# Another order of work for a gated mix of linear attention and a squared-ReLU layer

## Chip, cores and metric

The kernel runs on one core of a Trainium2 chip. The metric is the device time in microseconds (us) of one execution. Of the core's engines four compute here: TensorE (PE in the profile, with its weight loads as PEld), VectorE (DVE), ScalarE (ACT) and GpSimd (POOL). SyncE (SP) issues most of the DMAs.

## The reference

For 2048 rows `x` of width 448 in float32, the output mixes two branches row by row:

```python
g = sigmoid((x * gate_w).sum(-1, keepdims=True))
q, k, v = split(x @ wqkv)                     # 16 heads of 28
phi = lambda t: where(t > 0, t + 1, exp(t)) + 1e-6
kv  = einsum("bhsd,bhse->bhde", phi(k), v)    # sum over all 2048 rows
z   = sum of phi(k) over the rows
a   = (phi(q) @ kv / (phi(q) . z + 1e-6)) @ wo
b   = square(relu(x @ w1 + b1)) @ w2 + b2     # hidden width 1792
out = g * a + (1 - g) * b
```

The kernel does not form `v`. It sums `x^T phi(k)` over the rows (the "gram") and multiplies that by the `v` part of the weights once, then folds `kv` and `wo` into one matrix `m`.

## The kernel before

**Splitting.** A matrix product in float32 is made of three products of shorter numbers: each operand is split into a high part (rounded to `fp32r`) and a low part (what is left). Making the high part is a copy with a change of type (`split_hi`, lines 460 to 466); making the low part is a subtraction with two inputs (`split_lo`, line 468), which VectorE or GpSimd does.

**Two streams.** Every matmul uses 64 rows of the array, the lower half (`LO`) or the upper half (`UP`). Two streams of matmuls, one for each half, therefore run side by side. Both may add into the same bank of PSUM, but not at once. There are eight banks: four `acc` (outputs `o_ps` of the hidden layer's second product), two `mm` (first product, `h_ps`) and two `ms` (all else).

**Tiling and stages.** The rows are worked on in four blocks of 512 (`b` = 0 to 3) and 16 tiles of 128 (`t`); the hidden layer in 14 pieces of 128 columns (`f`). The first half of the kernel takes, for each block, the pieces 0 to 6 (`up` into `h_ps`, `hidden` on the other engines, `down` into `o_ps`), four key tiles (`keys`, `k_ps`) and four products of the gram (`gram`, `g_ps`). Between the halves stand `key_sums` (`z_ps`), `kv_product` (`kv_ps`) and `m_product` (`m_ps`), whose result goes through 32 DMAs on the POOL queue to `m_s`. The second half takes the blocks in the order 3, 0, 1, 2: pieces 7 to 13, the queries (`q_ps`), the denominators (`d_ps`) and the attention (`a_ps`).

**What follows each bank.** `hidden` (line 611) does ReLU and square on ScalarE, the high part on VectorE (`split_hi(dve, ...)`) and the low part on VectorE. `keys_done` (line 692) does an exponential, two VectorE operations for `phi`, the split of the key tile into `ph` and `pl`, adds the tile to `ksum` on GpSimd, and splits the raw `x` tile into `nh` and `nl`, with both subtractions on GpSimd (lines 700 to 709). `queries_done` (line 882) does `phi` and adds to the sum for the denominator; `denominators` (line 912) takes four reciprocals on VectorE and then splits the four query tiles (`scaled`).

**Who sets the order.** The class `Flow` is a planner that runs while the program is being written down. A call such as `dve.tensor_tensor(...)` only puts an operation into a list (`queue`, line 205), with an estimated duration (`cost`, line 218) and a rank (line 211: the planned time plus the patience of the step). `candidate` (line 235) picks for each engine, among the first 60 waiting operations, the one that can start first, and among equals the lowest rank. `product` (line 331) picks the next job of each matmul stream, looking up to 12 jobs ahead. The main loop (`run`, line 374) always carries out the earliest event. So the planner's estimates decide in which order each engine's instructions stand in the program. On the chip each engine then keeps that order and waits by semaphores; the planned times themselves have no effect there. The constants that feed the plan are on lines 32 to 34: time of one matmul of 512 or 448 columns, and the time from an engine's end to another's start.

**The first four products.** Line 991 gives the first four pieces of `h_ps` their banks: two from `mm`, and two from `ms`.

Of the kernel before, what the change touches and what calls it, by code (L numbers as in the profile page):

```python
# [16 lines left out]
P = 128  # L17
# [17 lines left out]
AFTER = mybir.DependencyInfo(mybir.DependencyClass.Sync, mybir.DependencyReason.DATA)  # L35

# [27 lines left out]
class Op:  # L64


    def __init__(self, emit, cost, after, rank, takes=None, size=0):
        self.emit, self.cost, self.after, self.rank = emit, cost, after, rank
        self.takes, self.size, self.end = takes, size, None

# [54 lines left out]
class Flow:  # L125
# [4 lines left out]
    def __init__(self, tc):  # L130
        self.tc, self.nc = tc, tc.nc
        self.tiles, self.queues, self.free, self.holds, self.kept, self.readers, self.shapes = {}, {}, {}, {}, {}, {}, {}
        self.now, self.patience, self.dma, self.switched = 0.0, 0.0, 1.3, -1.0
# [30 lines left out]
    def engine(self, name, unit):  # L164
# [3 lines left out]
        class Proxy:  # L168
            def __getattr__(self, method):
                return lambda *args, **kwargs: flow.queue(name, getattr(unit, method), method, args, kwargs)  # L170
        return Proxy()

# [32 lines left out]
    def queue(self, name, method, kind, args, kwargs):  # L205
        aps = [x for x in (*args, *kwargs.values()) if isinstance(x, View) or hasattr(x, "tensor")]
        out = kwargs.get("out", args[0] if args else None)
        parts = [(x, x is out) for x in aps]
        op = Op(lambda: method(*[real(x) for x in args], **{k: real(x) for k, x in kwargs.items()}),  # L209
                self.cost(name, kind, out, [x for x in aps if x is not out], args),  # L210
                {o for x, writes in parts for o in self.meeting(x, writes)}, self.now + self.patience,
                out.hold if isinstance(out, View) else None, free_size(out) * list(like(out).ap)[0][1] * 4
                if kind == "dma_start" else 0)
        for x, writes in parts:
            self.note(x, op, writes)
        self.queues[name].append(op)

    def cost(self, name, kind, out, ins, args):
        n = free_size(out)
        ps = any(like(x).space == PSUM for x in ins)  # L220
        wide = sum(free_size(x) > 1 for x in ins)
        if kind == "dma_start":
            return 0.54 if name == "pool" else 0.06
        if name == "act":
            f = args[2] if len(args) > 2 else None
            return {AF.Relu: 0.26, AF.Exp: 0.18}.get(f, 0.25 if ps and f else 0.205) + n * 0.000835
        if name == "pool":
            return 0.25 + n * 0.002 if wide > 1 else 0.4 + n * 0.001
        if kind == "reciprocal":
            return 0.13 + n * 0.006  # L230
        if kind == "memset":
            return 0.1
        return 0.155 + n / 960 if wide > 1 or ps else 0.1 + n * 0.00064

    def candidate(self, name):
        best = None
        for k, op in enumerate(self.queues[name][:60]):
            if any(x.end is None for x in op.after):
                continue
            start = max([self.free[name], self.now] + [x.end + SIGNAL for x in op.after])  # L240
            if op.takes is not None and op.takes.buffer is None:
# [3 lines left out]
                start = max(start, v[0])  # L245
            key = (max(start, self.free[name] + 0.05), op.rank)
            if best is None or key < best[0]:
                best = key, start, k
        return best and best[1:]

    def dispatch(self, name, k, start):
        op = self.queues[name].pop(k)
# [3 lines left out]
        self.tc.keep_in_program_order(op.emit())  # L256
        self.free[name] = op.end = start + op.cost
        if op.size:
            self.dma = max(self.dma, start + 0.6) + op.size / 385e3
            op.end = self.dma + LANDING  # L260

    def ready(self, j, s):
# [10 lines left out]
        if j.ready[s] is None:  # L275
# [3 lines left out]
            j.ready[s] = max([op.end + SIGNAL for op in wrote], default=0.0)  # L279
# [8 lines left out]
    def empty(self, tag):  # L288

        found = []  # L290
        for n, b in enumerate(self.banks[tag]):
            if b is None:
                found.append((0.0, n))
            elif b.end is not None:
                ops = [op.end for _, op, _ in self.tiles[b.ps.tensor.name]]
                if None not in ops:
                    found.append((max(ops) + SIGNAL, n))
        return min(found, default=None)

    def emit(self, j, s):  # L300
# [23 lines left out]
        if b.seen == b.total:  # L324
            b.end = self.stream[s]
            op = Op(None, 0.0, (), 0.0)
            op.end = b.end + LATE
            self.note(b.ps, op, True)
            b.done()
# [18 lines left out]
    def enter(self, n):  # L348
        while self.entered <= n + 1 and self.entered < len(self.steps):
            self.entered += 1  # L350
            self.patience = self.steps[self.entered - 1].patience
            if self.steps[self.entered - 1].before:
                self.steps[self.entered - 1].before()
# [834 lines left out]
```

## Time and profile before

| | us |
|---|---|
| median of 3 executions | 440.71 (440.56 to 440.78) |
| the profiled execution, its own time | 441.48 |
| span of the profiled execution, first to last instruction | 439.7 |

The span leaves 441.48 - 439.7 = 1.78 us of the execution's time outside. The granted clock of TensorE was 1.000 of full speed over the whole span. How to read the views: a matmul's record lasts longer than its share of the array, as two streams overlap, so the busy time of PE says little about how dense the matmuls are. The weight loads (PEld) are shorter, one for each matmul. In the timeline a row stands for one instruction or a run of like ones, and the brackets show what ended the idle time before.

### The profile page before, as it was taken

The page shows a single profiled execution, that of the slowest core. Times are in us where ns is not written, and L with a number is a line of the kernel's source. Part 1 is how long each engine was busy: PE and PEld are TensorE (multiplying, and loading weights), DVE is VectorE, ACT ScalarE, POOL GpSimd, SP SyncE. Part 2 cuts the span into 40 slices and gives each one's busy share as a digit, 9 for nine tenths or more (in the row PEclk, how much of TensorE's full clock was granted, in tenths as well). Part 3 has the DMA queues.
Part 4 walks back from the last instruction along what each step waited for, and adds up shares of the span by engine and source line. Part 5 has one row for each costly group of instructions (what it writes and reads, how often), then busy time and mean ns, then how long its engine had stood idle before and what let it go on. Part 6 is the DMA issues. An engine that isn't in the chain of part 4 may idle for free.

```text
span 439.7 us, 9349 instructions
## 1 busy us (share of the span) xinstructions
PE 433.8 (99%) x3978; PEld 413.3 (94%) x3978; DVE 268.5 (61%) x454; ACT 172.2 (39%) x298; POOL 67.5 (15%) x91
## 2 busy tenths in 40 slices
PE   8999999999999999999999999999999999999996
PEld 6899999999999999989999999999999899998995
DVE  4798525753587416783555849949535983458624
ACT  5846324532254214561533526415324242322530
POOL 0134104510065002530004900000000000000000
PEclk9999999999999999999999999999999999999999
DMA  7652210040111302223124631011210210001002
GB/s 255 240 152 87 76 46 25 23 138 25 41 59 45 113 3 66 83 84 92 41 86 112 110 92 49 0 64 34 62 49 1 85 25 1 0 33 55 1 1 83
DMA packets 17994, 29.02 MB, mean 66 GB/s; under 512 B 2544, under 2 KB 12448, under 8 KB 17952
## 3 DMA queue, kind: packets, MB, share of 16 engines
q1 hardware_dynamic: 16544, 26.81, 19.6%
q0 software_dynamic: 1408, 1.61, 2.2%
q8 instruction: 31, 0.51, 0.5%
q14 instruction: 11, 0.09, 0.1%
HBM read 22.08 MB, written 3.67 MB: 59 GB/s over the span
## 4 chain that ended last, share of the span: by engine, by line
PE 91%; DVE 5%; ACT 1%; DMA 1%; issue 0%; SPq 0%; DVEq 0%; ACTq 0%
PE h_ps L310 31%; PE o_ps L310 28%; PE a_ps L310 8%; PE g_ps L310 8%; PE k_ps L310 7%; PE q_ps L310 7%; DVE slot L209 4%; ACT slot L209 1%; PE kv_ps L310 1%; DMA slot<-in_xt 1%; DVE q L209 1%; PE m_ps L310 1%; PE d_ps L310 0%; ACT x L209 0%; PE z_ps L310 0%
## 5 line engine op out<-in xcount | busy, mean ns | idle before, releaser
L310 PE MATMUL h_ps<-x,w 64*128 64x512 f32 x1176 | 257.3, 394 | 0.4 <-ACT x L209 0.3
L310 PE MATMUL o_ps<-w_all,slot 64*128 64x448 f32 (+1 forms) x1332 | 240.5, 363 | 0.4 <-DVE slot L209 0.4
L310 PEld LDWEIGHTS o_ps<-w_all,slot 64*128 64x128 f32 (+1 forms) x1332 | 205.7, 184 | 6.5 <-DVE slot L209 1.8
L310 PEld LDWEIGHTS h_ps<-x,w 64*128 64x128 f32 x1176 | 193.6, 185 | 7.5 <-ACT x L209 0.8
L209 ACT ACTIVATE slot<-h_ps,few 128x512 f32<-128x512 f32 x56 | 38.0, 686 | 95.8 <-PE h_ps L310 83.8
L310 PE MATMUL q_ps<-x,wq_s 64*128 64x512 f32 x308 | 74.3, 393 | 0.0
L310 PE MATMUL k_ps<-wkm,x 64*128 64x450 f32 x336 | 66.3, 364 | 0.0
L209 DVE TENSOR_TENSOR slot<-slot,slot 128x512 fp32r<-128x512 f32 (+2 forms) x85 | 61.3, 733 | 4.4 <-DMA slot<-slot 1.7
L310 PE MATMUL a_ps<-wkm,q 64*128 64x448 f32 x336 | 62.2, 361 | 0.1
L310 PEld LDWEIGHTS k_ps<-wkm,x 64*128 64x128 f32 x336 | 57.0, 185 | 1.4 <-ACT slot L209 0.2
L310 PEld LDWEIGHTS q_ps<-x,wq_s 64*128 64x128 f32 x308 | 55.1, 184 | 1.5 <-DVE slot L209 0.3
L310 PEld LDWEIGHTS a_ps<-wkm,q 64*128 64x128 f32 x336 | 53.8, 184 | 1.3 <-DVE slot L209 0.6
L310 PE MATMUL g_ps<-p,nh 64*128 64x448 f32 x256 | 54.5, 359 | 0.0
L209 ACT ACTIVATE slot<-slot 128x512 f32<-128x512 f32 (+2 forms) x69 | 42.4, 625 | 14.7 <-DVE slot L209 13.8
L209 DVE CAST slot<-slot 128x512 fp32r<-128x512 f32 (+1 forms) x58 | 24.9, 430 | 31.9 <-ACT slot L209 30.7
L310 PEld LDWEIGHTS g_ps<-p,nh 64*128 64x128 f32 x256 | 40.6, 184 | 0.5
L209 POOL TENSOR_TENSOR nl<-slot,nh 128x384 fp32r<-128x384 f32 x16 | 19.3, 1209 | 117.6 <-ACT nh L209 117.6
L310 PE MATMUL g_ps<-p,nl 64*128 64x448 f32 x96 | 32.0, 360 | 0.0
L209 DVE SCALAR_TENSOR_TENSOR part<-part,gate,slot 128x448 f32<-128x448 f32 x13 | 8.8, 683 | 31.2 <-ACT slot L209 31.2
L209 ACT ACTIVATE slot<-a_ps,gate 128x448 f32<-128x448 f32 x16 | 10.0, 634 | 42.7 <-PE a_ps L310 40.7
L209 POOL TENSOR_TENSOR ksum<-ksum,slot 128x448 f32<-128x448 f32 x15 | 19.7, 1314 | 27.6 <-DVE slot L209 23.0
L209 DVE SCALAR_TENSOR_TENSOR slot<-slot,slot 128x448 f32<-128x448 f32 (+1 forms) x32 | 22.0, 688 | 1.7 <-ACT slot L209 1.5
(69 smaller groups left out, 350.0 us busy)
## 6 DMA issues: line engine op xcount, KB each, us to landing
slot<-in_xt SPq DMA_DIRECT2D x27, 256.0 KB, 2.8
slot<-in_xn SPq DMA_DIRECT2D x16, 224.0 KB, 2.5
out<-slot SPq DMA_DIRECT2D x16, 224.0 KB, 1.9
slot<-in_w SPq DMA_DIRECT2D x14, 224.0 KB, 2.8
slot<-in_w1a SPq DMA_DIRECT2D x8, 256.0 KB, 2.8
slot<-in_w1b SPq DMA_DIRECT2D x8, 192.0 KB, 4.0
wkm<-m POOLq DMA_DIRECT2D x24, 56.0 KB, 2.4
slot<-in_wq SPq DMA_DIRECT2D x4, 256.0 KB, 2.6
```

What stands on the lines that cost most here:

```text
L209: op = Op(lambda: method(*[real(x) for x in args], **{k: real(x) for k, x in kwargs.items()}), self.cost(name, kind, out, [x for x in aps ...
L310: ins = pe.matmul(b.ps[where or b.whole], real(a), real(m), start=b.seen == 1 + j.whole, stop=b.seen == b.total)
```

## The change

- **Three tables.** `SHIFT` adds to the rank of every operation that a bank or a step brings about (key: the bank's name or the step's), `MOVE` sorts the jobs of both matmul streams by step number plus an entry, `LEAVE` sets how willingly a copy goes to VectorE.
- **Copies to either engine.** `split_hi`, the copy of the query tile `c == 3` and the first copy into `gsum` are queued for ScalarE and VectorE at once (`either`); `candidate` compares when each would end, with 0.3 us (or the table's entry) added for VectorE. Whichever takes it removes it from the other's list. This holds for the copies of `hidden` too, which VectorE had, and for the other splits, which ScalarE had.
- **Key tiles.** The addition to `ksum` and both subtractions for `nl` and `nh` go from GpSimd to VectorE. GpSimd keeps the clearing and copies of `key_sums` and its DMAs.
[...]
- **Banks.** The third and fourth piece of the first four take `acc` banks instead of `ms` banks.
- **Conditions for the moved jobs.** `key_sums` waits for all key banks, `kv_product` for all gram banks, and a product that reads a block of `x` waits until all four chunks of it have been queued for splitting (`whole_x`).

The diff, cut to its core (each table with a few of its entries):

```diff
-C512, C448 = 0.2305, 0.204
+C512, C450, C448 = 0.2325, 0.2055, 0.2025
-LATE, SIGNAL, LANDING, HANDED = 0.25, 0.08, 1.9, 0.4
+LATE, SIGNAL, TO_PE, LANDING, HANDED = 0.17, 0.035, 0.09, 1.7, 0.22
+OVERLAP = {"act": 0.1, "dve": 0.085, "pool": 0.05, "sp": 0.0}
+SHIFT = {"a_ps1": 1.5, "a_ps10": 3, "a_ps13": -7.5, "d_ps1": 14.5, "g_ps0_0": 35, "k_ps1": 16, "k_ps10": 27.5,
...
+MOVE = {"a_ps10": 1.5, "a_ps11": -2.5, "a_ps12": 0.5, "a_ps14": 2.5, "a_ps9": 2.5, "d_ps0": 1, "d_ps1": -1.5,
+    "d_ps2": -0.5, "k_ps2": -5, "k_ps10": -3, "q_ps2_0": -4, "q_ps2_1": -3.5,
...
+LEAVE = {"a_ps10": 0.15, "a_ps14": -0.3, "h_ps0_0": 0.6, "h_ps0_1": 1, "h_ps0_10": 0, "k_ps0": 0.6,
...
+    def either(self, **calls):
+        self.queue({name: (getattr(unit, method), method, args, kwargs)
+                    for name, (unit, method, args, kwargs) in calls.items()})
...
+        op = Op({n: way(n, *call) for n, call in calls.items()},
+                {o for x in aps for o in self.meeting(x, x is out)},
+                self.now + self.patience + SHIFT.get(self.label, 0.0),
...
+        op.leave = LEAVE.get(self.label, 0.3)
...
+            if op.ways[name][2]:
+                start = max(start, self.port["pool" if name == "dve" else "dve"])
...
+        if best is not None and len(best[4].ways) > 1:
+            key, start, k, _, op, ready = best
+            ends = {n: max(ready, self.free[n]) + op.ways[n][1] + (op.leave if n == "dve" else 0.0) for n in op.ways}
+            best = key, start + ends[name] - min(ends.values()), k, start
...
-        self.jobs = [[(n, j) for n, step in enumerate(steps)
-                      for j in step.jobs[step.turn * s:] + step.jobs[:step.turn * s]] for s in range(2)]
+        self.jobs = [sorted([(n, j) for n, step in enumerate(steps)
+                             for j in step.jobs[step.turn * s:] + step.jobs[:step.turn * s]],
+                            key=lambda x: x[0] + MOVE.get(x[1].bank.name, 0.0)) for s in range(2)]
...
+    def copy(to, src):
+        flow.either(act=(nc.scalar, "activation", (to, src, AF.Copy), {}), dve=(nc.vector, "tensor_copy", (to, src), {}))
+
     def split_hi(eng, hi, src):
-        if eng is act:
-            act.activation(hi, src, AF.Copy)
-        elif eng is pool:
-            pool.tensor_scalar(hi, src, 1.0, 0.0, op0=ALU.mult, op1=ALU.add)
-        else:
-            eng.tensor_copy(hi, src)
+        copy(hi, src)
...
-        if t == 0:
-            pool.tensor_copy(ksum, p)
+        if not pend:
+            dve.tensor_copy(ksum, p)
         else:
-            pool.tensor_tensor(ksum, ksum, p, op=ALU.add)
+            dve.tensor_tensor(ksum, ksum, p, op=ALU.add)
...
-        split_lo(pool, nl, raw[:, :384], nh[:, :384])
-        split_lo(pool, nh[:, D:], raw[:, 384:], nh[:, 384:D])
+        split_lo(dve, nl, raw[:, :384], nh[:, :384])
+        split_lo(dve, nh[:, D:], raw[:, 384:], nh[:, 384:D])
...
-                act.copy(gsum[c], bank.ps[:, :D])
+                copy(gsum[c], bank.ps[:, :D])
...
-            act.copy(v, ps)
+            copy(v, ps)
...
-    first = [up_bank(0, f, *((mm_p, "mm") if f < 2 else (ms_p, "ms"))) for f in range(4)]
+    first = [up_bank(0, f, *((mm_p, "mm") if f < 2 else (acc_p, "acc"))) for f in range(4)]
```

More of the change, by code (lines that the diff above doesn't have):

```diff
@@ L64, with __init__ @@
 class Op:
-    def __init__(self, emit, cost, after, rank, takes=None, size=0):
-        self.emit, self.cost, self.after, self.rank = emit, cost, after, rank
+    def __init__(self, ways, after, rank, takes=None, size=0):
+        self.ways, self.after, self.rank = ways, after, rank
         self.takes, self.size, self.end = takes, size, None
+        self.leave = 0.0
 class Hold:
@@ L203, in note, with queue, way @@
                 x.hold.uses.append(op)
-    def queue(self, name, method, kind, args, kwargs):
+    def queue(self, calls):
+        (name, (_, kind, args, kwargs)), *_ = calls.items()
         aps = [x for x in (*args, *kwargs.values()) if isinstance(x, View) or hasattr(x, "tensor")]
         out = kwargs.get("out", args[0] if args else None)
[L208 to L211, printed above, removed]
+        n = next(k for k, x in enumerate(aps) if x is out)
+        ins = aps[:n] + aps[n + 1:]
+        def way(name, method, kind, args, kwargs):
+            return (lambda: method(*[real(x) for x in args], **{k: real(x) for k, x in kwargs.items()}),
+                    *self.cost(name, kind, out, ins, args))
+        op = Op({n: way(n, *call) for n, call in calls.items()},
+                {o for x in aps for o in self.meeting(x, x is out)},
+                self.now + self.patience + SHIFT.get(self.label, 0.0),
@@ L227, in cost @@
         if name == "pool":
-            return 0.25 + n * 0.002 if wide > 1 else 0.4 + n * 0.001
+            return 0.25 + n * 0.002 if wide > 1 else 0.4 + n * 0.001, wide > 0
         if kind == "reciprocal":
-            return 0.13 + n * 0.006
+            return 0.13 + n * 0.0063, False
         if kind == "memset":
-            return 0.1
-        return 0.155 + n / 960 if wide > 1 or ps else 0.1 + n * 0.00064
+            return 0.1, False
+        plain = not ps and all(len([k for _, k in list(like(x).ap)[1:] if k > 1]) < 2 for x in (out, *ins))
@@ L235, in candidate @@
+        if wide > 1 or not plain:
+            return 0.06 * scaled + 0.155 + n / 960, wide > 1 and not ps
+        return 0.06 * scaled + 0.093 + n * 0.00064, n > 8
     def candidate(self, name):
@@ L239, in candidate @@
                 continue
-            start = max([self.free[name], self.now] + [x.end + SIGNAL for x in op.after])
+            ready = max([self.now] + [x.end + SIGNAL for x in op.after])
+            start = max(self.free[name], ready)
             if op.takes is not None and op.takes.buffer is None:
@@ L278, in ready @@
                 return None
-            j.ready[s] = max([op.end + SIGNAL for op in wrote], default=0.0)
+            j.ready[s] = max([op.end + TO_PE for op in wrote], default=0.0)
         t = max([self.stream[s], j.ready[s], self.left.get((o, j.bank), 0.0)] + [x.end for x in j.after])
@@ L605, in whole_up @@
         low, high = [], []
+        if x_key(b, f) not in whole_x:
+            raise KeyError
         for c in range(4):
@@ L689, in keys @@
         bank.done = lambda: keys_done(t, bank.ps)
-        return [Job(bank, lambda: key_terms(t), C448, [("x", t // 4, False), "wk"])]
+        return [Job(bank, lambda: key_terms(t), C450, [("x", t // 4, False), "wk"])]
     def keys_done(t, ps):
@@ L775, in key_sums_job @@
         bank.done = lambda: sums_done(bank.ps)
-        return [Job(bank, key_sums, 0.07, ["zk"], [key_banks[NT - 1]])]
+        return [Job(bank, key_sums, 0.224, ["zk"], list(key_banks.values()))]
     kv, wv_s, kvm = [], [], []
@@ L818, in kv_product @@
     def kv_product():
-        return [Job(kv_bank, kv_terms, 0.19, ["wv"], [grams[NB - 1, c] for c in range(4)])]
+        return [Job(kv_bank, kv_terms, 0.196, ["wv"], list(grams.values()))]
     wo_raw, wo_s = {}, {}
```

67 lines of the change are left out of this document (44 added, 23 removed), and 44 rows, old and new, of tables (LEAVE, MOVE, SHIFT).

## The prediction

> **What bounds the kernel now.** I read the page's busy times and chain first.
>
> ```profile
> PE 433.8 (99%) x3978; PEld 413.3 (94%) x3978; DVE 268.5 (61%) x454; ACT 172.2 (39%) x298; POOL 67.5 (15%) x91
> ...
> PE 91%; DVE 5%; ACT 1%; DMA 1%; issue 0%; SPq 0%; DVEq 0%; ACTq 0%
> ```
>
> TensorE is the bound: 91% of the chain of work that ended last is matmuls, and the number of matmuls is the same after the change. So a gain can only come from stretches in which the two streams of matmuls are thinner than they could be. PE's 99% hides these, because records of the two streams overlap: while one stream waits, the other still shows as busy. The view of windows shows them, by the count and busy time of the weight loads (PEld, the second group of numbers in a row; VectorE's is the third).
>
> ```profile
> 0.00:11.00 11.00, 9.64 (x60) 7.04 (x62) 5.43 (x14) 5.98 (x10) 0.39 (x6) 1.00 0.78 255
> 11.00:22.00 11.00, 11.00 (x84) 9.10 (x82) 7.75 (x15) 9.51 (x18) 1.12 (x2) 1.00 0.65 239
> 22.00:44.00 22.00, 22.00 (x212) 21.63 (x210) 19.42 (x32) 11.77 (x23) 9.14 (x10) 1.00 0.40 120
> 44.00:66.00 22.00, 22.00 (x213) 21.64 (x212) 8.79 (x15) 6.40 (x11) 1.54 (x1) 1.00 0.20 61
> ...
> 132.00:154.00 22.00, 21.94 (x208) 21.17 (x207) 13.01 (x21) 7.80 (x14) 6.09 (x6) 1.00 0.28 79
> 154.00:176.00 22.00, 22.00 (x213) 21.69 (x211) 8.96 (x16) 6.26 (x11) 2.99 (x3) 1.00 0.12 34
> 176.00:198.00 22.00, 21.94 (x199) 20.57 (x197) 17.75 (x26) 13.05 (x23) 9.13 (x9) 1.00 0.27 84
> ...
> 260.00:282.00 22.00, 21.63 (x188) 19.64 (x185) 20.23 (x35) 12.69 (x21) 0.00 (x0) 1.00 0.20 55
> ...
> 326.00:348.00 22.00, 21.62 (x195) 20.32 (x193) 14.27 (x24) 8.95 (x16) 0.00 (x0) 1.00 0.15 54
> ...
> 392.00:414.00 22.00, 21.96 (x198) 20.11 (x196) 18.81 (x33) 9.17 (x16) 0.00 (x0) 1.00 0.12 44
> 414.00:440.00 26.00, 22.07 (x191) 20.76 (x187) 7.86 (x13) 4.80 (x8) 0.00 (x0) 1.00 0.10 36
> sum 440.00, PE 433.80 PEld 413.34 DVE 268.52 ACT 172.22 POOL 67.52; mean PE 20.66 PEld 19.68 DVE 12.79 ACT 8.20 POOL 3.22
> ```
>
> In three windows (22:44, 44:66, 154:176) nothing is missing: 21.65 us of weight loads and 211 of them in 22 us, 9.6 a us. I take 21.65 of 22 (0.984) as full. Against it are missing: 0:11 10.82 - 7.04 = 3.8 us; 11:22 1.7; 132:154 0.5; 176:198 1.1; 260:282 2.0; 326:348 1.3; 392:414 1.5; 414:440 25.6 - 20.8 = 4.8. Over the whole row of sums 433.0 - 413.3 = 19.7 are missing, so 19.7 - 16.7 = 3.0 lie in the windows not shown. Most of 0:11 and 414:440 is the start (waiting for the first loads) and the last results and stores, which no order removes. What an order of work can win is thus some 1.7 + 0.5 + 1.1 + 2.0 + 1.3 + 1.5 = 8.1 us in six places, and parts of the 3.0 and of the end.
>
> By PE's own row (433.8 of 439.7) only 5.9 us would be idle, nearly all at the start, and nothing could be won. [...]
>
> **The change part by part.** Durations are of the profiled execution, 441.48 us (span 439.7 and 1.78 outside); it lies 0.77 above the median of 440.71, and I take the sum off both alike.
>
> *A. Banks of the third and fourth product.*
>
> ```profile
> 14.77 1.99 PE L310 MATMUL h_ps<-x,w 64*128 64x512 f32 x10
> 16.58 3.65 PE L310 MATMUL k_ps<-wkm,x 64*128 64x450 f32 x20
> ...
> 15.84 1.26 ACT L209 ACTIVATE slot<-h_ps,few 128x512 f32<-128x512 f32 x2 [1.43 <-PE h_ps L310]
> ...
> 18.03 1.26 ACT L209 ACTIVATE slot<-h_ps,few 128x512 f32<-128x512 f32 x2
> ...
> L209 DVE TENSOR_TENSOR wkm<-slot,wkm x4: 619/620/625, 13.4 to 15.1; 128x450 fp32r<-128x450 f32 x3, 64x450 fp32r<-64x450 f32 x1
> ```
>
> The key product `k_ps` needs an `ms` bank, and both hold `h_ps` until ScalarE's ReLU has read them. The first ReLUs start at 15.84, the first key matmul at 16.58, and in 3.65 us only 20 matmuls go out where 35 would fit: a second key tile has no bank until a later ReLU, and two streams can't share one bank. The key weights are ready from 15.1 + 0.62 = 15.7. With `acc` banks for those two products, both `ms` banks are free and two key tiles start side by side when the first products run out. The 15 matmuls are worth 15 / 9.6 = 1.6 us, and 14.77 to 16.58 has a few more. What is late next is `o_ps`, which needs the same two `acc` banks, but it needs the low part of the first hidden piece first, which is later than the ReLU. I take **-1.5** (0 to -1.7, all that is missing in 11:22).
>
> *B. Key-tile work from GpSimd to VectorE.*
>
> ```profile
> 192.59 1.53 DVE L209 TENSOR_TENSOR slot<-slot,slot 128x512 fp32r<-128x512 f32 x1
> ...
> 192.56 1.02 POOL L209 TENSOR_TENSOR nl<-slot,nh 128x384 fp32r<-128x384 f32 x1 [5.36 <-ACT nh L209]
> 193.54 0.78 POOL L209 TENSOR_TENSOR nh<-slot,nh 128x64 fp32r<-128x64 f32 x1
> ...
> 191.25 2.98 PE L310 MATMUL h_ps<-x,w 64*128 64x512 f32 x15
> 193.75 0.67 PE L310 MATMUL o_ps<-w_all,slot 64*128 64x448 f32 x2
> ...
> L209 POOL TENSOR_TENSOR ksum<-ksum,slot 128x448 f32<-128x448 f32 x15 | 19.7, 1314 | 27.6 <-DVE slot L209 23.0 <-PE o_ps L310 3.9 <-DVE few L209 0.6
> L209 POOL TENSOR_TENSOR nl<-slot,nh 128x384 fp32r<-128x384 f32 x16 | 19.3, 1209 | 117.6 <-ACT nh L209 117.6
> L209 DVE TENSOR_TENSOR p<-slot,p 128x448 fp32r<-128x448 f32 x16 | 17.2, 1076 | 4.6 <-ACT p L209 4.5
> L209 DVE TENSOR_TENSOR q<-slot,q 128x512 fp32r<-128x512 f32 x16 | 10.3, 685 | 0.2
> L209 DVE TENSOR_TENSOR w<-slot,w 128x384 fp32r<-128x384 f32 x6 | 3.4, 608 | 0.0
> L209 DVE TENSOR_TENSOR slot<-slot,slot 112x448 fp32r<-112x448 f32 x5 | 3.0, 619 | 0.2
> L209 DVE TENSOR_TENSOR w<-slot,w 64x128 fp32r<-64x128 f32 x3 | 0.9, 287 | 0.1
> ```
>
> The subtraction that gives a hidden piece's low part takes 1.53 us here, beside two GpSimd subtractions, where the same shape takes 0.685 with GpSimd idle (row `q`). For those 0.84 us the next `o_ps` matmuls wait: only 15 `h_ps` matmuls go out in 2.98 us, one stream alone. `p` suffers likewise, 1.076 against 0.619. So VectorE gets, for each of 16 tiles, 0.61 (`nl`) + 0.29 (`nh`, by the nearest narrow row) + 0.62 (`ksum`) = 1.5 us, 24 in all, and gets back 16 x 0.457 = 7.3 on `p` alone. None of the moved results is wanted soon: GpSimd now takes 1.3 and 1.2 us for each and nothing on the page waits for `ksum`. Of 1.1 + 0.5 us missing in 176:198 and 132:154 I take **-1.2** (0 to -1.5).
>
> The cover for the new work is VectorE's idle time: 8.8 of 22 us busy in 44:66, 9.0 in 154:176. It is thin in 22:44: 19.4 busy, with 10 of the 48 moved operations, 3.3 tiles. 19.4 + 3.3 x 1.5 - 3.3 x 0.46 = 22.9 of 22. What relieves it is the next part.
>
> *C. Copies to either engine.*
>
> ```profile
> L209 DVE CAST slot<-slot 128x512 fp32r<-128x512 f32 x56 | 24.6, 438 | 31.9 <-ACT slot L209 30.7 <-issue 0.8
> L209 ACT ACTIVATE x<-slot 128x512 fp32r<-128x512 f32 x20 | 12.2, 621 | 3.8 <-DMA slot<-in_xt 3.8
> ```
>
> The copies of `hidden` take 0.44 on VectorE and about 0.62 on ScalarE, which is idle 10 of 22 us in 22:44. Three of them moved bring VectorE there to 21.6 of 22: full, but not over. I add **+0.6** for stalls in this stage (the 22.9 - 22 = 0.9 with no relief, 0 with all of it). A copy that goes the slower way makes its hidden chain 0.2 later; the chain starts a piece ahead of its use, so this costs nothing while the streams have other jobs.
>
> *D. The order itself, in the denominators' stages.*
>
> ```profile
> 260.68 0.69 DVE L209 TENSOR_TENSOR slot<-slot,slot 128x512 fp32r<-128x512 f32 x1 [0.70 <-ACT slot L209]
> ...
> 266.37 3.38 DVE L209 RECIPROCAL slot<-slot 128x128 f32<-128x128 f32 x4
> 269.66 0.63 DVE L209 TENSOR_SCALAR slot<-q_ps 128x512 f32<-128x512 f32 x1
> 270.21 2.48 DVE L209 TENSOR_TENSOR slot<-slot,slot 128x512 f32<-128x512 f32 x4
> 272.61 1.89 DVE L209 TENSOR_TENSOR q<-slot,q 128x512 fp32r<-128x512 f32 x3
> ...
> L310 PEld LDWEIGHTS a_ps<-wkm,q x336: 182/184/188, 278.0 to 431.1; 64*128 64x128 f32 x168
> ```
>
> At 260:282 the bound is VectorE, 20.2 of 22 busy: the last low part for `d_ps` ends at 261.4, reciprocals, products and splits run one after the other from 266.4 to 276, and only then can attention start, at 278.0. The same run of work stands at 326:348 and 392:414. The totals there, 2.0 + 1.3 + 1.5 = 4.8 us, are waits for the order, not for lack of VectorE as a whole (61% busy). `MOVE` puts work there that the streams can do meanwhile: `q_ps2_0` and `q_ps2_1` come 4 and 3.5 steps earlier, so that their phi is done before `d_ps2`; `a_ps12`, `a_ps14`, `a_ps9` and `a_ps10` come 0.5 to 2.5 steps later; casts can leave VectorE. The chain of 0.69 + 0.75 + 3.38 + 2.48 + 1.89 us itself stays. I take half: **-2.4** (+1.0 to -4.4; above zero if a moved query chain lands on another busy stage).
>
> *E. The rest.* Of the 3.0 us in windows not shown some is short gaps that return wherever streams change jobs: **-0.7** (0 to -1.5). At the end one tile's order can shift: **-0.5** (+0.5 to -1.0). New constants alone change nothing on the chip but the order.
>
> *F. POOL's DMAs.*
>
> ```profile
> L209 POOL DMA_DIRECT2D wkm<-m x32: 494/501/803, 235.1 to 253.1; - x32
> ```
>
> The last is issued at 253.1, 25 us before attention reads `m_s` at 278.0; casts on VectorE ran beside them already, and the longest issue took 0.80. I take 0. [...]
>
> Sum: -1.5 - 1.2 + 0.6 - 2.4 - 0.7 - 0.5 = **-5.7**. The profiled execution would come to 435.8, the median to 440.71 - 5.7 = **435.0**.
>
> **The rivals.**
>
> 1. *Gains of A and B alone.* Engines keep the planned order strictly; a plan with less slack (0.17 us from a matmul's end instead of 0.25) may turn planned gaps into unplanned ones. For it: 260:282 shows VectorE full, whatever its order. Against: VectorE is half idle in most windows. 440.71 - 2.7 = 438.0, up to 440 if 22:44 adds 2.
> 2. *VectorE becomes the bound in the key stages (slower).* Each tile's 1.5 us stands ahead of a hidden piece's cast and low part. It decides once the streams have less than 1.5 us of other matmuls ready. In 22:44 that is 3.3 tiles, 5.0 us; three more such tiles (176:198 has 17.8 of 22 busy) 4.5. With the gains without the 0.6: 440.71 - 6.3 + 9.5 = 443.9. For it: 22.9 of 22. Against: casts can leave, and after 44 VectorE has 13 us free.
> 3. *Nothing to win.* Were PE's 99% the truth, the time stays at 440.7. Against: 188 matmuls where 213 fit.
> 4. *The order does nearly all it can:* 1.7 + 1.5 + 4.4 + 1.0 + 0.6 = 9.2, so 431.5.
>
> **How the numbers follow.** Forecast (433 to 437.8) 0.55; rival 4 and below 433 0.15; rival 1 (437.8 to 439.8) 0.15; rival 3 0.05; slower, by rival 2 and the DMAs, 0.10. A measurement of this kernel tells about 0.2% (0.9 us) from no change. Faster 0.85, same 0.05, slower 0.10. The range 431.5 to 440.0 runs from rival 4 to rival 1 with a full 22:44.
>
> **What would show it.** A: 84 matmuls in 11:22 become over 95, key matmuls pair up from the start. B: no GpSimd subtraction, `p` at about 0.62 and no VectorE subtraction of 512 columns over 0.8. C: casts of `hidden` on ScalarE; VectorE below 22 in 22:44 with PEld still 21.6. D: PEld above 20.6 in each of the three stages. Wrong it would be with PEld below 21 in 22:44, or with the missing 8 us found again in other windows.

## The result, and the profile after

| | before | after |
|---|---|---|
| median, same chip (us) | 440.75 (440.56 to 441.08) | 435.93 (435.43 to 436.02) |
| ratio of the times | | 0.9888, 95% interval 0.987 to 0.9905 |
| the profiled execution (us) | 441.48 | 435.88 |
| its span (us) | 439.7 | 434.0 |

The change saves 4.8 us; 5.7 were forecast. The page of the kernel after, busy time and share of the span for each engine:

```profile
PE 428.1 (99%) x3978; PEld 413.0 (95%) x3978; DVE 257.7 (59%) x479; ACT 187.8 (43%) x321; POOL 18.0 (4%) x43
```

The same 3978 matmuls with the same weight loads (413.0 us against 413.3) stand in a span shorter by 5.7 us. VectorE took over GpSimd's 48 operations and still is busy for 10.8 us less: 45 copies of `hidden` left it, and its operations are short again where they had been long beside GpSimd's (`p` takes 0.618 us in the mean for 1.076; both below). The windows of the kernel after, cut at the same times as before (length; busy time and count of PE, PEld, DVE, ACT and POOL; granted clock):

```profile
11.00:22.00 11.00, 11.00 (x103) 9.72 (x99) 10.33 (x20) 9.92 (x19) 0.00 (x0) 1.00 0.83 308
22.00:44.00 22.00, 21.67 (x207) 20.68 (x205) 18.07 (x42) 11.93 (x22) 0.00 (x0) 1.00 0.45 131
...
132.00:154.00 22.00, 22.00 (x208) 21.31 (x206) 8.15 (x15) 8.68 (x15) 0.00 (x0) 1.00 0.08 24
...
176.00:198.00 22.00, 22.00 (x211) 21.64 (x210) 17.54 (x39) 11.41 (x22) 0.00 (x0) 1.00 0.45 132
...
238.00:260.00 22.00, 21.73 (x194) 19.97 (x193) 15.06 (x26) 9.51 (x16) 8.97 (x19) 1.00 0.37 72
260.00:282.00 22.00, 22.00 (x204) 21.63 (x203) 21.72 (x37) 11.86 (x21) 0.00 (x0) 1.00 0.15 43
...
304.00:326.00 22.00, 22.00 (x208) 21.64 (x206) 8.74 (x15) 9.32 (x16) 0.00 (x0) 1.00 0.23 67
326.00:348.00 22.00, 21.95 (x199) 21.36 (x197) 17.21 (x28) 9.78 (x17) 0.00 (x0) 1.00 0.10 39
...
392.00:414.00 22.00, 22.00 (x204) 21.50 (x202) 15.87 (x26) 11.22 (x19) 0.00 (x0) 1.00 0.12 43
```

By the prediction's own measure (0.984 of a window's length less PEld) the changes in what is missing (us) are as follows, with the counts of weight loads beside them:

| window | missing before | after | loads before | after |
|---|---|---|---|---|
| 11:22 | 1.7 | 1.1 | 82 | 99 |
| 22:44 | 0.0 | 1.0 | 210 | 205 |
| 132:154 and 176:198 | 1.6 | 0.4 | 404 | 416 |
| 238:260 | 0.3 | 1.7 | 203 | 193 |
| 260:282, 326:348, 392:414 | 4.8 | 0.5 | 574 | 602 |

The three denominators' stages gave 4.4 us. By counts it is less: 602 weight loads instead of 574, and 28 / 9.6 = 2.9 us. At 11:22 it is the other way round: 0.6 us by busy time, 17 / 9.6 = 1.8 by counts. The busy time is the looser of the two. A run with other tables (e7 below) has in 304:326 the same 206 loads as the kernel after, and 1.5 us less of busy time:

```profile
304.00:326.00 22.00, 22.00 (x207) 20.15 (x206) 8.08 (x14) 8.72 (x15) 0.00 (x0) 1.00 0.22 61
```

So 1.5 us can be "missing" by that measure though no load is. Loads of the two streams overlap, and an overlap counts once: 206 loads of 0.184 us in the mean are 37.9 us, and they show as 21.64 busy. Between two executions of the same program (after, and e11 below) a window behind the first 11 us differs by up to 0.6 us in busy time and by up to 3 in count. Losses that were not there before, at 22:44 (1.0 by busy time, 0.5 by counts) and at 238:260 (1.4 and 1.0), took about half of the denominators' gain back.

The groups of the kernel after that answer to steps B, C and F (busy, mean ns of one, idle time before):

```profile
L274 DVE TENSOR_TENSOR p<-slot,p 128x448 fp32r<-128x448 f32 x16 | 9.9, 618 | 0.0
L274 DVE TENSOR_TENSOR ksum<-ksum,slot 128x448 f32<-128x448 f32 x15 | 9.3, 621 | 0.2
L274 DVE TENSOR_TENSOR nl<-slot,nh 128x384 fp32r<-128x384 f32 x16 | 8.8, 552 | 0.0
L274 DVE TENSOR_TENSOR nh<-slot,nh 128x64 fp32r<-128x64 f32 x16 | 3.5, 218 | 0.0
L274 DVE CAST slot<-slot 128x512 fp32r<-128x512 f32 x11 | 4.7, 426 | 12.9 <-ACT slot L274 12.8
L274 POOL DMA_DIRECT2D wkm<-m x32 | 16.0, 509 | 34.5 <-ACT m L274 23.6 <-DVE m L274 9.7 <-DMA wkm<-m 1.1
```

The moved work costs 0.62 + 0.55 + 0.22 = 1.39 us a tile (1.5 was taken), `p` is back at 0.618 from 1.076, 45 of the 56 copies of `hidden` have left VectorE, and POOL's DMAs take 0.51 each as before.

Where do the new losses come from? Around 22 us the timeline of the kernel after (start, duration; in brackets the idle time before and what ended it) shows:

```profile
21.10 0.62 DVE L274 TENSOR_SCALAR slot<-k_ps 128x448 f32<-128x448 f32 x1
21.81 0.98 ACT L274 ACTIVATE slot<-k_ps 128x448 f32<-128x448 f32 x2 [0.68 <-DVE slot L274]
22.39 0.16 DVE L274 COPY few<-k_ps 128x1 f32<-128x1 f32 x1 [0.67 <-ACT slot L274]
...
22.60 0.47 PE L402 MATMUL k_ps<-wkm,x 64*128 64x450 f32 x1 [0.33 <-DVE few L274]
```

Three reads of `k_ps`, on two engines, and each waits for the one before: ScalarE 0.68 us for VectorE, VectorE 0.67 us for ScalarE, and the matmul that needs the bank for the copy of one column. None needs the other's result; each is held by a semaphore of the program until the read before it has ended, and the planner does not count that. Such waits are not new: in the kernel before, that copy of one column waits for ScalarE in seven places, 4.5 us in all, here in three, 1.9 us. The same pattern stands at the head of the other loss, 238:260, with ScalarE's read of `q_ps` held until VectorE's has ended:

```profile
237.82 0.69 DVE L274 TENSOR_SCALAR slot<-q_ps 128x512 f32<-128x512 f32 x1 [3.63 <-PE q_ps L402]
...
238.61 0.60 ACT L274 ACTIVATE slot<-q_ps 128x512 f32<-128x512 f32 x1 [2.48 <-DVE slot L274]
```

The traces show these waits, 0.68 and 0.67 us above, and not what they guard against; no run here lifts them.

### The profile page after: what moved, and what is told of

Read it like the earlier page. It is cut to its first block, busy times and chain, and to the rows that moved or that the text cites. A ratio compares the mean times of both kernels' runs of the same rounds, so it can differ in the third digit from the quotient of the medians.

```text
span 434.0 us, 9343 instructions
## 1 busy us (share of the span) xinstructions
PE 428.1 (99%) x3978; PEld 413.0 (95%) x3978; DVE 257.7 (59%) x479; ACT 187.8 (43%) x321; POOL 18.0 (4%) x43
## 4 chain that ended last, share of the span: by engine, by line
PE 92%; DMA 2%; ACT 2%; DVE 2%; SPq 1%; issue 0%; ACTq 0%
PE h_ps L402 31%; PE o_ps L402 29%; PE q_ps L402 9%; PE g_ps L402 8%; PE a_ps L402 7%; PE k_ps L402 7%; DVE slot L274 2%; ACT slot L274 1%; DMA slot<-in_w1a 1%; DMA slot<-in_w 1%; PE kv_ps L402 1%; SPq L274 1%; PE d_ps L402 1%; PE m_ps L402 1%; ACT w L274 0%
## 5 line engine op out<-in xcount | busy, mean ns | idle before, releaser
L402 PE MATMUL h_ps<-x,w 64*128 64x512 f32 x1176 | 243.3, 394 | 0.0
L402 PE MATMUL o_ps<-w_all,slot 64*128 64x448 f32 (+1 forms) x1332 | 219.7, 362 | 0.0
L402 PEld LDWEIGHTS o_ps<-w_all,slot 64*128 64x128 f32 (+1 forms) x1332 | 191.3, 184 | 3.6 <-issue 0.3
L402 PEld LDWEIGHTS h_ps<-x,w 64*128 64x128 f32 x1176 | 188.7, 185 | 5.3 <-DVE x L274 0.7
L274 ACT ACTIVATE slot<-slot 128x512 f32<-128x512 f32 (+2 forms) x114 | 70.9, 628 | 12.9 <-DVE slot L274 4.3
L402 PE MATMUL q_ps<-x,wq_s 64*128 64x512 f32 x308 | 67.2, 394 | 0.2 <-ACT slot L274 0.2
L402 PE MATMUL g_ps<-p,nh 64*128 64x448 f32 x256 | 60.3, 360 | 0.0
L274 ACT ACTIVATE slot<-q_ps 128x512 f32<-128x512 f32 x16 | 9.6, 598 | 30.4 <-PE q_ps L402 25.4
L274 ACT ACTIVATE slot<-k_ps 128x448 f32<-128x448 f32 x16 | 8.5, 542 | 28.3 <-PE k_ps L402 13.0
L274 DVE TENSOR_TENSOR x<-slot,x 128x512 fp32r<-128x512 f32 (+1 forms) x29 | 19.1, 668 | 1.4 <-ACT x L274 1.1
```

Of the source, the lines that this page charges most:

```text
L274: return (lambda: method(*[real(x) for x in args], **{k: real(x) for k, x in kwargs.items()}), *self.cost(name, kind, out, ins, args))
L402: ins = pe.matmul(b.ps[where or b.whole], real(a), real(m), start=b.seen == 1 + j.whole, stop=b.seen == b.total)
```

## The experiments

All times are medians, all ratios to the kernel before on the same chip (440.86 to 441.04 us in the three sets). Only e9, e10 and e12 ran beside the unchanged kernel after (e11); the others are set against its 435.93 us from another set.

| run | us | ratio (95%) |
|---|---|---|
| e3: all but the tables | 440.32 | 0.9992 (0.9981 to 1.0003) |
| e7: `MOVE` alone of the tables | 438.28 | 0.994 (0.9928 to 0.9952) |
| e8: the tables without `MOVE` | 440.45 | 0.9993 (0.9977 to 1.0009) |
| e12: the old constants | 437.16 | 0.9905 (0.9886 to 0.9925) |
| e1: key-tile work on GpSimd, places kept | 436.54 | 0.9904 (0.9891 to 0.9916) |
| e2: before, with key-tile work on VectorE | 440.17 | 0.9989 (0.9979 to 0.9999) |
| e5: copies on the engines of before | 437.01 | 0.9908 (0.9894 to 0.9923) |
| e4: before, with the new banks | 450.49 | 1.0234 (1.0196 to 1.0272) |
| e6: after, with the old banks | 442.4 | 1.0027 (1.0008 to 1.0046) |
| e11: after, unchanged | 435.7 | 0.9882 (0.986 to 0.9904) |
| e9: planner knows readers of a bank | 436.29 | 0.9884 (0.9864 to 0.9904) |
| e10: e9 and tables searched anew | 434.89 | 0.9861 (0.9836 to 0.9887) |

The intervals are 0.2 to 0.5% wide (e4's 0.8%), so a difference of 1.5 us or less between two rows is not settled by the times alone; the windows have to carry it.

### What the tables are worth (step D)

e3 empties the three tables and makes the queries wait until the sum of the keys has been planned.

```diff
-SHIFT = {"a_ps1": 1.5, "a_ps10": 3, "a_ps11": 3, "a_ps13": -7.5, "a_ps14": 6, "a_ps2": -3, "a_ps4": 1.5, "a_ps5": -1.5,
...
+SHIFT = {}
+MOVE = {}
+
+LEAVE = {}
...
-        return [Job(bank, lambda: query_terms(b, c), C512, [x_key(b, NH)])]
+        return [Job(bank, lambda: query_terms(b, c), C512, [x_key(b, NH)], [key_banks["sum"]])]
```

> The changed kernel with the three tables empty: new estimates, copies to either engine, key tiles on VectorE and the new banks stay, and queries wait for the key sums (without the tables the plan would have them read the sums too early). Theory (the tables bring part D, the denominators' stages, and E, some 3.6 us by the prediction, and the rest the other parts): 438.0 to 440.0, with the missing weight loads in the denominators' windows as before (1 to 2 us each). Rival (the measured durations and free copies alone give a good order): within 1 of 435.9.

Measured: 440.32, no difference from before, and just outside the range of the theory. Everything in the change but the tables, together, is worth nothing that can be measured; the tables hold 440.3 - 435.9 = 4.4 of the 4.8 us. The windows of e3 say how that comes about:

```profile
238.00:260.00 22.00, 21.99 (x193) 20.27 (x191) 13.07 (x22) 9.87 (x17) 9.75 (x20) 1.00 0.41 67
260.00:282.00 22.00, 22.00 (x204) 21.36 (x203) 22.00 (x37) 11.04 (x19) 0.00 (x0) 1.00 0.19 60
...
326.00:348.00 22.00, 22.00 (x201) 21.21 (x199) 17.49 (x28) 11.54 (x20) 0.00 (x0) 1.00 0.11 42
348.00:370.00 22.00, 20.61 (x195) 19.22 (x193) 10.59 (x18) 8.26 (x14) 0.00 (x0) 1.00 0.06 13
...
392.00:414.00 22.00, 22.00 (x202) 20.74 (x201) 17.48 (x28) 11.02 (x18) 0.00 (x0) 1.00 0.12 44
```

The expectation was that the denominators' windows would be as empty as before. They are not: 260:282, 326:348 and 392:414 have 603 weight loads with no table at all, against 602 in the kernel after and 574 in the kernel before. But 238:260 lost 1.1 against before (21.39) and 348:370 lost 1.9 (21.15). A new plan fills one hole and opens another. The kernel after has holes too (238:260 is no better there, 19.97); its holes add up to less. Against e3 its gain lies above all in 348:370 (211 loads for 193), 176:198 (210 for 201) and 11:22 (99 for 92).

e7 and e8 divide the tables (`SHIFT = {}` and `LEAVE = {}` in the one, `MOVE = {}` in the other).

> The changed kernel with MOVE alone; SHIFT and LEAVE are empty. With all three empty it took 440.3, so the tables carry 4.4 us. Theory D (the order of the matmul jobs, above all queries earlier and attention later, is what fills the denominators' windows): 436.5 to 438, with less than 0.7 us of weight loads missing in each of 260:282, 326:348 and 392:414. Rival (the ranks of the other engines' operations carry it): 438.5 to 440.5.

> The changed kernel with SHIFT and LEAVE and without MOVE: the mirror of the run with MOVE alone. Theory D: 438.5 to 440.5, missing weight loads at the denominators as without tables. Rival (ranks carry it): 436.5 to 438. If both runs come out near 438 or both near 440, the gain belongs to the combination.

Measured: `MOVE` alone 438.28, 2.0 less than e3 (which has the queries' condition besides) and between its two expectations. `SHIFT` and `LEAVE` alone 440.45, nothing. Yet on top of `MOVE` they bring 438.3 - 435.9 = 2.4 more. The parts do not add up; they are one set of entries for one plan. The largest loss of e8 against the kernel after stands in 238:260 (162 loads for 193), in the windows and the waits around 245 us; the next, in 392:414, is smaller (193 for 202). The profiled execution took 442.26, 1.8 more than the median:

```profile
244.50:247.00 2.50, 0.62 (x6) 0.18 (x2) 1.64 (x4) 1.68 (x4) 1.48 (x3) 1.00 0.57 98
247.00:251.00 4.00, 3.90 (x22) 3.52 (x24) 3.90 (x9) 1.18 (x2) 3.66 (x7) 0.61 0.49 80
```

```profile
DVE m L261 <- DMA wkm<-m: 4.8, 1, 4.8
...
PEld q_ps L389 <- DVE m L261: 2.4, 1, 2.4
```

A query product was put behind `m_ps` in the same bank; `m_ps` is read out by VectorE into a buffer that POOL's DMAs must leave first, 4.8 us; so no weight load goes out for 2.4 us. And then the streams run at a granted clock of 0.61 for 4 us. That second part is not in every execution: of the twelve, two show a mean granted clock of 0.994 and 0.995 (this one and one of 443.06), the other ten 0.998 to 1.000.

e12 keeps the tables and puts back the constants of the kernel before.

```diff
-C512, C450, C448 = 0.2325, 0.2055, 0.2025
+C512, C450, C448 = 0.2305, 0.204, 0.204
...
-LATE, SIGNAL, TO_PE, LANDING, HANDED = 0.17, 0.035, 0.09, 1.7, 0.22
+LATE, SIGNAL, TO_PE, LANDING, HANDED = 0.25, 0.08, 0.08, 1.9, 0.4
```

> The changed kernel, tables and all, with the constants for matmuls, ends and landings of the kernel before. Nothing else of the program depends on them but the order. Theory (the tables are steps from one particular plan, and with other estimates they act on another): 438 to 441. Rival (the tables hold a good order by themselves): within 1 of 435.9.

Measured: 437.16, that is 1.5 above the unchanged kernel beside it, so between the two expectations; the two intervals overlap. Three windows of e12:

```profile
22.00:44.00 22.00, 21.99 (x211) 21.31 (x209) 18.46 (x42) 11.95 (x22) 0.00 (x0) 1.00 0.49 139
...
66.00:88.00 22.00, 22.00 (x200) 20.37 (x198) 8.67 (x19) 8.04 (x15) 0.00 (x0) 1.00 0.09 24
...
238.00:260.00 22.00, 22.00 (x205) 21.74 (x203) 14.41 (x24) 9.74 (x16) 15.36 (x30) 1.00 0.72 141
```

A hole opened at 66:88 (198 loads, 212 in the kernel after), and the two new losses of the kernel after, 22:44 and 238:260, are filled. The tables keep most of their worth under other constants, in another order.

### Which engine does the key-tile work (step B)

e1 leaves every instruction of the kernel after in its place in the program and lets GpSimd issue the 48 key-tile operations. e2 does the reverse with the kernel before.

The first tile's copy into `ksum` and the two subtractions are changed likewise; the diffs show one line of the four.

```diff
...
-            dve.tensor_tensor(ksum, ksum, p, op=ALU.add)
+            flow.queue({"dve": (nc.gpsimd.tensor_tensor, "tensor_tensor", (ksum, ksum, p), {"op": ALU.add})})
...
```

```diff
...
-            pool.tensor_tensor(ksum, ksum, p, op=ALU.add)
+            flow.queue("pool", nc.vector.tensor_tensor, "tensor_tensor", (ksum, ksum, p), {"op": ALU.add})
...
```

> The changed kernel with its order of every engine kept, but the 48 key-tile operations (ksum, nl, nh) issued by GpSimd again, at the places where VectorE had them. [...] Rival (these operations burden VectorE, which is nearly full in the key stages): the time falls, below 435.5. Rival (the gain is all in the order): within 0.5 of 435.9.

> The kernel before with its order of matmuls, ScalarE and DMAs kept, but the 48 key-tile operations issued by VectorE, at the places of the program where GpSimd had them. Theory B: the 1.53 us subtraction before the stall at 193 becomes 0.7, and the time falls by 0.7 to 1.5 us, to 439.3 to 440.0. Rival (VectorE becomes the bound at 22 to 44, where it then has 22.9 us of work in 22): the time rises by 1 us or more, above 441.7.

Measured: e1, 436.54, costs 0.6 us against after. If `p` is long again beside GpSimd and matmuls wait for it, as step B has it, the author had expected 437 to 438; the rival that sees all in the order goes to 436.4, and e1 lies between; e2, 440.17, gains 0.7 against before, just short of its range. Both orders give the same small answer, at the edge of what the intervals tell. Now the place that step B named. The timeline of e2, where the prediction saw 15 matmuls of one stream in 2.98 us beside a subtraction of 1.53, and its window:

```profile
189.94 2.99 PE L310 MATMUL h_ps<-x,w 64*128 64x512 f32 x15
...
191.26 0.68 DVE L209 TENSOR_TENSOR slot<-slot,slot 128x512 fp32r<-128x512 f32 x1
...
192.44 0.67 PE L310 MATMUL o_ps<-w_all,slot 64*128 64x448 f32 x2
```

```profile
176.00:198.00 22.00, 21.94 (x200) 20.95 (x198) 15.40 (x34) 12.67 (x22) 0.00 (x0) 1.00 0.29 91
```

The subtraction is down to 0.68 us and the 15 matmuls still take 2.99: the stretched subtraction was there, but it did not hold the stream. The window is hardly better for it (198 weight loads for 197, 20.95 us for 20.57). And in e1, with `p` stretched again to 1.05 us in the mean, the same window is full; of the two stages the first suffers (199 loads, 205 in the kernel after):

```profile
22.00:44.00 22.00, 21.24 (x200) 19.99 (x199) 18.24 (x29) 12.00 (x22) 10.81 (x12) 1.00 0.39 114
...
176.00:198.00 22.00, 22.00 (x211) 21.55 (x209) 19.47 (x30) 11.35 (x22) 11.61 (x11) 1.00 0.45 131
```

So 176:198 was mended by the new order, not by the engine: 209 loads with GpSimd's help against 210 without. What held one stream there in the order of before stays open; a wait for the other half's bank (0.5 us, `h_ps` for `h_ps`, in the waits of the kernel before and of e2) is near it, but was not tested.

### The copies (step C)

e5 keeps the places and sends each copy to the engine that it had before.

```diff
+        self.last = op
...
-    def copy(to, src):
+    def copy(to, src, eng=None):
+        made = (nc.vector.tensor_copy, (to, src)) if eng is dve else (nc.scalar.activation, (to, src, AF.Copy))
...
+        op = flow.last
+        op.ways = {n: (lambda: made[0](*[real(x) for x in made[1]]), *way[1:]) for n, way in op.ways.items()}
...
-        copy(hi, src)
+        copy(hi, src, eng)
```

> The changed kernel with the places of every operation in the program kept, but each copy issued by the engine that had it in the kernel before: the casts of hidden on VectorE, the other splits' copies on ScalarE. Theory C (the free choice is needed because VectorE took over the key tiles): VectorE is late in its full stages (22:44, 260:282), and the time rises by 1 to 4 us over 435.9, to 437 to 440. Rival (copies are off the path, either engine will do): within 0.5 of 435.9.

Measured: 437.01, 1.1 us more than after, at the lower edge of the theory's range. Its windows:

```profile
22.00:44.00 22.00, 21.13 (x196) 19.87 (x198) 17.88 (x42) 11.21 (x21) 0.00 (x0) 1.00 0.41 118
...
260.00:282.00 22.00, 22.00 (x203) 20.66 (x201) 21.97 (x38) 10.70 (x19) 0.00 (x0) 1.00 0.16 37
```

At 22:44 the weight loads fall from 205 to 198, where step C expected it. At 260:282 they fall from 203 to 201 only; the busy time (21.63 to 20.66) says more, but e11, the kernel after once more, has 21.12 there, so this place is not clear. Nor is VectorE the reason at 22:44: it is no busier than in the kernel after (17.88 us against 18.07), with as many operations (42). Who makes a copy matters there; that it helps by taking work off VectorE is not shown.

### The banks of the third and fourth product (step A)

e4 changes the banks alone in the kernel before; e6 undoes them alone in the kernel after, tables kept. Both plans are made anew.

```diff
-    first = [up_bank(0, f, *((mm_p, "mm") if f < 2 else (ms_p, "ms"))) for f in range(4)]
+    first = [up_bank(0, f, *((mm_p, "mm") if f < 2 else (acc_p, "acc"))) for f in range(4)]
```

> The kernel before with only the banks changed: third and fourth first product in acc instead of ms; the planner, unchanged, then makes the rest of the order anew. Theory A: the gap at 15 to 19 closes, the window 11:22 has over 95 matmuls, and the time falls by 1.2 to 1.7 us, to 439.0 to 439.5. Rival (the four acc banks are then short for o_ps, so the gap only moves): within 0.5 of 440.75.

> The changed kernel with the third and fourth first product back in ms banks, tables kept, the rest planned anew. Theory A, as the run with the banks alone left it (the acc banks pay only in an order that fits them, and the order pays only with the banks): the key products wait again at 15 to 19, 11:22 has fewer than 92 matmuls, and the time rises by 1.5 to 2 us or more, to 437.5 to 441. Rival (the banks are worth nothing with the order so far improved): within 0.5 of 435.9.

Measured: e4 takes 450.49, slower than before by 9.6 us; step A had forecast 1.5 faster. Windows of e4 (the profiled execution took 448.84; the mean granted clocks of all six lie between 0.985 and 0.996):

```profile
11.00:22.00 11.00, 10.30 (x89) 8.93 (x86) 10.08 (x21) 9.93 (x20) 0.00 (x0) 1.00 0.82 297
...
176.00:198.00 22.00, 21.26 (x186) 19.36 (x184) 16.40 (x24) 10.33 (x19) 8.74 (x9) 1.00 0.29 84
...
238.00:260.00 22.00, 18.52 (x143) 16.47 (x142) 10.76 (x20) 6.43 (x12) 15.97 (x32) 0.84 0.62 120
```

At the start the gain is 4 weight loads, not 15: the hole moves from 16 us to 19.5 to 21.8. And two stages that have nothing to do with these banks lose 1.2 (20.57 to 19.36) and 4.9 us (21.39 to 16.47). The large one is the same trap as in e8, in the timeline:

```profile
248.19 0.54 ACT L209 ACTIVATE m<-m_ps 128x448 fp32r<-128x448 f32 x1 [1.20 <-DMA wkm<-m]
...
250.45 0.61 DVE L209 TENSOR_TENSOR m<-m_ps,m 128x448 fp32r<-128x448 f32 x1
...
251.11 1.22 PE L310 MATMUL q_ps<-x,wq_s 64*128 64x512 f32 x2 [3.48 <-DVE m L209]
...
252.13 0.62 PE L310 MATMUL q_ps<-x,wq_s 64*128 64x512 f32 x1
```

A product of the first microseconds was planned otherwise, every later choice fell otherwise, and 230 us later a query product stood behind `m_ps`. e6 shows the other direction: 442.4, 6.5 more than after. Not all of this is order: five of its twelve executions, with a mean granted clock of 0.998 or 0.999, took 440.3 to 441.2; the other seven, at 0.992 to 0.995, took 442.4 to 444.5. Its window at the start, of an execution of 441.16:

```profile
11.00:22.00 11.00, 10.18 (x75) 7.68 (x73) 10.09 (x21) 10.23 (x20) 0.00 (x0) 1.00 0.89 293
```

73 loads against 99: here the `ms` banks do what step A read from the page, and worse (the first weight load of a key product waits 1.26 us for ScalarE). The wait is real, but its price depends on the plan around it. That a bank takes the matmuls of one stream at a time is a condition of the planner (`ready`, line 266 of the kernel before); no run lifts it.

### The new stalls

e11 is the kernel after once more. e9 adds to the planner that two engines' reads of one bank stand one after the other, with the tables as they are; e10 has in addition new table entries, found by a random search for an earlier end of the plan (183 of the entries of `SHIFT`, 91 of `MOVE` and 111 of `LEAVE` differ).

```diff
+        self.readings = {}
...
+        op.bank = next((x.tensor.name for x in aps if not isinstance(x, View) and x.space == PSUM), None)
...
-            ready = max([self.now] + [x.end + SIGNAL for x in op.after])
+            ready = max([self.now] + [x.end + SIGNAL for x in op.after]
+                        + [end + SIGNAL for n, end in self.readings.get(op.bank, ()) if n != name])
...
+        if op.bank is not None:
+            self.readings.setdefault(op.bank, []).append((name, op.end))
```

> The changed kernel once more, beside the next three on the same chip: 435.4 to 436.2.

> The changed kernel with one rule more in its planner: two engines that read the same PSUM bank are planned one after the other (in the changed kernel's trace ScalarE's exponential starts only when VectorE's read of the same key bank has ended, and VectorE's next read waits for it, 0.7 us each, at 21 to 22.6). Tables kept, so the order is another one that they were not made for. Theory (a plan that knows the wait loses less on the chip, but the tables fit the old plan): 435.5 to 437.5. Rival (the rule alone saves the waits): 434 to 435.4.

> The same planner rule, with entries of the three tables changed by a random search for an earlier end of the plan. Theory (what is lost between plan and chip at 22, 238, 256 and 336, some 2 us, comes largely from planned reads of one bank at once): 434.0 to 435.3, with those gaps smaller. Rival (they come from DMA and engine times that the plan has wrong anyway): 435.5 to 436.5.

Measured: 435.7, 436.29 and 434.89, each in its range (for e9 and e10 that of the theory). The windows of e9, and those of e10:

```profile
22.00:44.00 22.00, 22.00 (x211) 21.57 (x209) 19.25 (x45) 10.35 (x19) 0.00 (x0) 1.00 0.48 140
...
110.00:132.00 22.00, 22.00 (x202) 21.06 (x200) 15.41 (x36) 9.41 (x17) 0.00 (x0) 1.00 0.14 38
```

```profile
22.00:44.00 22.00, 22.00 (x212) 21.45 (x210) 18.16 (x43) 13.27 (x25) 0.00 (x0) 1.00 0.36 110
...
238.00:260.00 22.00, 22.00 (x201) 21.12 (x199) 16.22 (x28) 10.62 (x18) 11.99 (x25) 1.00 0.63 131
```

In e9 the loss at 22:44 is gone (21.57 against 20.68), and around 22 us neither of the two waits of 0.7 us is there; but 110:132 now lacks 0.6 (200 loads for 208), and the time stays. That fits the waits of readers as the cause of the loss, but does not show it: e9 is a new order as a whole, and e12, whose planner does not know the rule, fills 22:44 and 238:260 as well. With entries searched for the planner with the rule (e10), 22:44 and 238:260 are both better than in the kernel after (21.45 and 21.12 against 20.68 and 19.97). e10 is the lowest time of all, 0.8 below the unchanged kernel beside it, yet the two intervals overlap: that it beats the changed kernel is likely and not shown. Nor was the same search made without the rule, so what the rule itself brings stays open.

## Why the prediction was right, and where it was not

Direction and size were right, 435.0 against 435.9. Window by window the sum was close too, as the bullets show; but the experiments show that what filled a window was mostly not the step that the sum named for it. That the total came within 0.9 us is in part luck: the loss at 238:260, which no step foresaw, was made up by D's windows and those not shown, which gave more than was forecast.

- **What bounds the kernel: held.** The weight loads stay at 413 us, and the 5.7 us of the span came out of the holes that the windows showed. Of the two signs of being wrong that the text named, one came true, PEld below 21 in 22:44 (20.68), and one in part: missing time was found again in other windows, 2.4 us of it (1.0 in 22:44, 1.4 in 238:260), in e3 all of it within the noise, in e4 more than all. The measure itself, busy time of weight loads, was looser than the text took it to be; the counts are the safer reading.
- **D, order in the denominators' stages (-2.4): the windows filled as forecast, but not by the tables.** The three windows gave between 2.9 (counts) and 4.4 us (busy time); the step took half of the 4.8 that was missing there. It named `MOVE` as what would fill them. e3 has no table and 603 weight loads in these windows against 602, so the rest of the change, planned anew, fills them; what the tables are worth (4.4 us) lies elsewhere, in holes that the new plan would otherwise have. The reading that VectorE bounds 260:282 was off: it is busy for 21.72 of 22 us there after the change too, and the weight loads for 21.63. The streams had lacked other work, not VectorE time.
- **A, banks (-1.5): the step that failed as a term of a sum.** 11:22 went from 84 to 103 matmuls, as foreseen (over 95), and its 17 more weight loads are 1.8 us. But e4 shows that the banks alone cost 9.6 us and gain 4 loads, and e6 that, within the new plan, going back costs 4.4 us or more. A local edit under a greedy planner has no price of its own.
- **B, key tiles (-1.2): right sign, half the size, wrong cause.** By e1 and e2 it is worth 0.6 to 0.7. The two windows did improve by 1.2, just the forecast, which would have seemed to prove the step; e1, with GpSimd back and 176:198 still full, shows that this was the order. What VectorE gets back was mis-sized as well: the step counted 7.3 us, on `p` alone. In e2 the moved operations take 22.0 us and VectorE's whole busy time still falls by 3.0 (268.5 to 265.6), so 25 us came back; the low parts of `hidden`, for one, go from 758 to 683 ns in the mean.
- **C, copies (+0.6): right place and size, other cause.** 22:44 lacks 1.0 (0.5 by counts), and not by a full VectorE (18.07 of 22, where the step had 21.6). The readers of one bank that wait for each other stand at the head of the loss; that they cause it is likely, not shown. With the copies on the engines of before it lacks 1.8 (e5).
- **E (-1.2):** the windows not shown gave some 1.6 together, of which the step had 0.7; 238:260 took 1.4. The end gave nothing: after 414 us 25.3 - 20.8 = 4.5 us were missing before, and 19.7 - 15.0 = 4.7 after.
- **F, POOL's DMAs (0): held**, 0.507 us against 0.501 in the median. The chance of 0.10 for slower counts the DMAs too; no run shows them as a cause: the longest issue took 0.64 us after and 0.80 before.
- **Rival 2 (VectorE as the bound):** refuted by e2: with the key-tile work, VectorE's busy time in 22:44 fell from 19.42 to 17.86, where the step had 22.9, since its operations were short again without GpSimd's (`p` 0.621 us in the mean for 1.076). **Rival 1** had A and B as sure gains, and neither is. **Rival 3** falls with the result. **Rival 4** (431.5) was not reached; the best order here, e10, takes 434.9.

## What to carry to other kernels

Where a program plans the order of its own instructions, price no part of an edit by itself: make the plan again with that part alone and look at all windows, since a change at 15 us can open a hole at 245. A window that improves by the forecast amount proves no cause; put the suspected operation back, in the same place, and see whether the hole comes back. With two streams side by side, compare windows by the count of weight loads before their busy time, and profile the same program twice to see how far a window moves by itself. Before tuning an order, look in the trace for waits that the planner does not know (here two engines reading one bank, 0.7 us each time at 22 us); whether teaching it those pays is open here.

## What the runs showed of the hardware

**After a full stop the granted clock was lower in two profiles, and not in a third.** In the profiled execution of e8 both streams stood without a matmul for 2.0 us (the row of 244.5 to 247 above has 0.62 busy, and the next matmul starts at 247.10), and the granted clock of 247 to 251 is 0.61; in e4, after 3.5 us, a matmul of 512 columns takes 0.62 us where it took 0.39, the next in its stream starts 0.43 us later (0.23 before the stop), and the windows of e4 read:

```profile
246.00:251.00 5.00, 1.64 (x13) 1.07 (x10) 4.32 (x9) 3.75 (x7) 3.00 (x7) 0.87 0.50 82
251.00:255.00 4.00, 3.89 (x17) 3.09 (x18) 3.29 (x7) 0.00 (x0) 3.65 (x8) 0.50 0.45 69
255.00:260.00 5.00, 5.00 (x41) 4.46 (x40) 0.00 (x0) 0.00 (x0) 3.76 (x8) 0.85 0.58 100
```

In these rows 0.13 x 5 + 0.50 x 4 + 0.15 x 5 = 3.4 us of clock are missing. The streams were slower with it: 18 weight loads in 4 us at 0.50 are 4.5 a us, and e8's 24 in 4 us at 0.61 are 6.0, where 9.6 are full. So up to 3.4 us are lost on top of the stop, by an estimate from these rows. In e3 a stop of 1.39 us cost no clock (348:370 shows 1.00 above). The runs give no sharp length beyond which a stop costs clock, and none changes the stop alone, so that it brings the clock down is likely, not shown. After the 2.0 us at most two of e8's twelve executions lost clock, as the other ten have mean clocks of 0.998 to 1.000, and the 0.61 over 4 us alone would leave 0.996 of 440 us.

**The start differs from one execution to the next.** The same instructions (after and e11) ran these matmuls of 512 columns between 7.4 and 10 us (count; shortest, median and longest in ns), first after, then e11:

```profile
L402 PE MATMUL h_ps<-x,w x22: 385/391/496, 7.2 to 9.8; 64*128 64x512 f32 x22
```

```profile
L402 PE MATMUL h_ps<-x,w x16: 625/626/628, 6.8 to 9.8; 64*128 64x512 f32 x16
```

e11's take 0.626 us, as long as e4's 0.62 at a granted clock of 0.50, although the view of windows shows 1.00 for both. In after, the last one that long starts at 6.5 us, in e11 at 9.8. In the first 11 us e11 has 48 weight loads and after 60; at 9.6 a us the 12 are 1.25 us, by estimate. That profiled execution of e11 took 437.74 us, after's 435.88; e11's others took 435.3 to 436.4. So the 1.00 that the view shows for the first microseconds does not tell how long a matmul took there, and one profile's first 11 us are no base for a claim of 1 us.
